# A different fixed order for the first third of a written-out instruction plan (banded attention and a gated product, one core)

## The chip, the cores and the metric

The kernel runs on one core of one Trainium2 chip. The metric is the device time of one execution in microseconds. The kernel before takes 804.42 us, the median of three runs that lie between 804.17 and 805.79 us.

## The reference

Eight batches of eight heads, head width 64. Each head has 512 local tokens and 32 global ones. A global query attends to all 544 keys of its head. A local query attends to the 32 global keys and to the local keys at most 32 positions away. The attention output, laid out as 4352 tokens of 512 features, goes through a gated product.

```python
s_g = scale * q_g @ k_all.T;      out_g = softmax(s_g) @ v_all
s_l = [scale * q_l @ k_g.T, where(|i - j| <= 32, scale * q_l @ k_l.T, -1e9)]
out_l = softmax(s_l) @ [v_g, v_l]
x = concat([out_g, out_l]) as (4352, 512)
a = x @ w1;  b = x @ w2           # 512 -> 1024
out = ((a * b) @ w3) @ w_out      # 1024 -> 1024 -> 512
```

All inputs and outputs are fp32.

## The kernel before, in words

Products that must keep fp32 precision are split: a tensor is rounded to a short "hi" part and the remainder is the "lo" part, and three matmuls (hi*hi, lo*hi, hi*lo) replace one. `hi_of` (L423) is a copy, `lo_of` (L426) a subtraction of hi from the source; nearly every hi or lo may run on more than one engine. The first batch (heads 0 to 7) uses plain fp32 matmuls instead.

The work is cut into 3878 numbered steps (`add` makes them), each a call that issues a few instructions on one engine. The ones that the prediction names:

- `sp m` on TensorE: the scores of a pair of heads (L497, 16 matmul records). `mmax n e` and `exps n e`: the masked minimum of a block of scores on VectorE (L506) and its exponential on ScalarE (L510).
- `own n`, `turn n` on VectorE: 32x32 block transposes of head n (tiles `tw`, `TT`); `eh`/`el`, `hi`/`lo`, `me`: hi and lo parts of the transposed weights (tiles `TT`, `PT`, `G`).
- `av n x` on TensorE (L637, L644): the values of head n. `cb n x`: a copy of half of its result. `sum n x` (L658): the sum of the two halves.
- `kph`/`kpl`, `vh`/`vl`: hi and lo parts of keys and values. `sg`, `cg`, `mg`: the scores of the global queries.
- `fetch`, `unit kind a e step` (L849 to L853, L423, L426): a weight block arrives packed and is unpacked in steps 0 (VectorE), 2 (ScalarE), 3 (VectorE), 4 (hi) and 5 (lo, tile `w12l`). 32 blocks of 512 KB (`raw`, three buffers) come first, then 16 of 256 KB (`w12s m e`, tile `raw_w12s`, three buffers of the ring `o`); a buffer is fetched again only after the unpacking of the block three before it has ended.
- `fold t j` (L929): the product of w3 and w_out, made on the chip. `w34h`/`w34l`: its hi and lo parts.
- `first k m s` (L795 to L797, 12 matmuls): block m of w1 (s = 0) or w2 (s = 1) for 256 tokens k; where the tokens' last pair of heads is late, nine of the 12 are a step of their own, `begin k m s`, and `first` has three. Blocks m = 4 to 7 need the four `w12s m e`. `ga`, `gb` (L805), `gh`, `gl`: the gate. `second k m` (L827 to L829): the last product. `out`, `store`: the result.

What decides the order is one string, `PLAN`: 3878 words such as `790S` or `844V`, a step's number and the engine that it runs on (P TensorE, A ScalarE, D VectorE, V GpSimd, S the DMA queue of SyncE).

```python
    for w in PLAN:
        n, e = int(w[:-1]), names[w[-1]]
        assert e in steps[n][1] and all(place[k] in seen for k in after.get(steps[n][0], ()))
```

`list_schedule` walks the string; each engine gets its steps in the order in which they stand and runs them strictly in that order. A step waits for the steps that it depends on (`after`), buffers included. The costs at the top of the file take no part once the string is written out. A few `idle_products` (L368) run on TensorE while nothing else can, at the start.

Of the kernel before, what the change touches and what calls it, by code (L numbers as in the profile page):

```python
# [30 lines left out]
def i(ap):  # L31
# [39 lines left out]
    1V 790S 386S 328S 3V 387P 791S 792P 0S 3877V 388D 390S 793D 8S 391P 5V 794A 795D 392D 797D 799D 796A 393A 12S 800A  # L71
    10A 394D 329S 13D 9D 395P 798A 396D 14A 152S 11D 397A 801P 805A 16S 808A 15D 389S 158S 803D 807V 813P 804D 806A 17D
    814D 802A 18A 809P 20S 816D 248P 818D 815A 811P 817A 19D 820D 846S 819A 258P 22A 21D 821A 810A 23D 845S 825P 827D
    24S 812A 829A 826A 828D 28S 26A 32S 249P 830D 822D 831A 25D 832A 27D 30A 399S 29D 36S 259P 847P 833P 848D 835P 31D
    850D 34A 868D 852D 834A 863A 870D 40S 854D 851A 849A 872D 250P 260P 33D 874D 853A 251P 400P 37D 855A 38A 398S 862A
    35D 875A 39D 856P 823S 859A 403S 858D 860D 261P 836D 857A 44S 330S 861A 42A 252P 864P 869A 873A 41D 48S 866P 871A
    43D 262P 46A 401D 879P 404P 52S 45D 837D 47D 49D 50A 54A 263P 159D 885A 899S 51D 883A 880A 253P 56S 405D 884D 264P
    2V 406A 900S 254P 53D 58A 55D 881A 876D 57D 331V 882A 60S 255P 265P 865D 901P 59D 886A 407D 256A 887P 257D 922D
    867A 64S 62A 266A 61D 902D 824S 877S 924D 954S 65D 888A 63D 268P 889P 269P 66A 904D 839V 154A 68S 67D 903A 408P
    270P 842V 906D 267D 923A 271P 278P 926D 72S 905A 409A 925A 916A 838V 70A 907A 69D 890A 908D 878S 272P 333V 153D 74A  # L80
    909A 928D 843A 71D 273P 402S 155D 410A 891V 76S 73D 274P 275P 844V 276D 953S 910P 913D 927A 893V 929A 80S 279P 277D
    915A 917A 894A 912A 892V 914A 280P 334V 933P 911D 918P 78A 75D 82A 77D 920P 281P 936A 332D 937A 895V 79D 840A 934D
    81D 282P 412S 896D 160A 935D 938A 288P 84S 930D 86A 164S 841D 289P 955P 413A 83D 85D 88S 87D 161D 939A 92S 919A 96S
    90A 976D 335S 283P 290P 166A 956D 958D 978D 960D 414V 957A 931S 940A 284P 94A 89D 285P 7V 959A 291P 921A 962D 91D
    98A 93D 961A 100S 941P 95D 97D 943P 942D 415P 979A 286A 336V 944A 980D 104S 416A 292P 102A 963A 165D 293P 99D 294P
# [12 lines left out]
    201D 1035A 3097A 3103P 181D 189D 1038A 1036D 1060S 422V 3104P 1064V 190A 1039D 1063A 194S 1091A 191D 1055A 450S
    3098D 1053A 1000V 1099D 1098D 442P 1056V 192A 1054V 1066S 202A 1051A 193D 195D 1052D 3105A 3099P 196A 1102A 451A
    197D 1100S 203D 3111P 1067P 434S 198A 1070P 204A 1068A 1103D 1121A 206S 199D 205D 435A 1156S 1069D 3106D 452V 207D  # L100
    1071A 1072D 208A 436V 1105A 437A 209D 443A 1122D 3100P 1096A 1073V 1094A 1104A 444D 210A 1050S 438V 211V 1132D
    3107A 3113P 1106S 218S 1131D 3112P 212S 1097V 1157P 3108D 219D 1135A 1158D 220A 1101S 3115A 1107S 1095V 214A 221D
    3109P 1188D 1133S 1136V 3110P 1160D 213D 222A 223D 1159A 224S 215D 1092A 1162D 1190D 1164D 3114P 3116D 1161A 1123S
    1093V 1078V 1163A 225D 1139S 216A 1108P 1165A 1111P 1192D 217V 1194D 226A 1109A 236S 3117A 1138A 1129A 1112A 1075V
    1134S 1110D 227D 228A 1137A 1127A 3118V 1173D 3121P 1113D 237D 1172D 230S 229V 453P 1130V 454A 455D 1128V 238A
    1140S 1125A 456A 239D 3119P 3123P 1126D 1141P 1176A 240A 457D 231D 232A 1189A 458D 242S 1144P 1177V 1142A 1174S
    1124S 1145A 244A 338S 243D 3120P 1143D 1146D 1193A 241V 466S 245D 246A 233D 247D 234A 1191A 1195A 1231P 235D 1179A
    1147V 459S 1178A 1180S 3122P 1175S 445S 1232D 3125A 1205D 339V 1206D 1234D 3124P 3135P 467V 1209A 3136P 1166A 3126D
    1074V 1148V 3127A 446A 460S 340V 1079A 1235A 1236D 1210D 1207S 3137P 341V 3139A 1238D 1167V 1262D 1076A 1264D 1181S
# [1364 lines left out]
```

## Time and profile before

| | |
|---|---|
| median of three runs | 804.42 us |
| the profiled execution | 803.93 us |
| its span | 802.2 us |
| granted TensorE clock | 1.00 throughout |
| TensorE matmuls busy | 791.2 us, 99% of the span |
| VectorE busy | 524.7 us, 65% |
| ScalarE busy | 455.2 us, 57% |
| GpSimd busy | 394.0 us, 49% |

The span runs from the first to the last instruction of the profiled execution; 1.7 us of its time lie around it. An engine's busy time leaves out waiting, issuing and branches. The shares are means over stages that differ: the first 110 us hold the folding of the weights and the first batch, up to 155 us the unpacking of the small weight blocks runs beside the first gated products, and after that the same pattern repeats.

### The profile page before, as it was taken

The page shows a single profiled execution, that of the slowest core. Times are in us where ns is not written, and L with a number is a line of the kernel's source. Part 1 is how long each engine was busy: PE and PEld are TensorE (multiplying, and loading weights), DVE is VectorE, ACT ScalarE, POOL GpSimd, SP SyncE. Part 2 cuts the span into 40 slices and gives each one's busy share as a digit, 9 for nine tenths or more (in the row PEclk, how much of TensorE's full clock was granted, in tenths as well). Part 3 has the DMA queues.
Part 4 walks back from the last instruction along what each step waited for, and adds up shares of the span by engine and source line. Part 5 has one row for each costly group of instructions (what it writes and reads, how often), then busy time and mean ns, then how long its engine had stood idle before and what let it go on. Part 6 is the DMA issues. An engine that isn't in the chain of part 4 may idle for free.

```text
span 802.2 us, 17177 instructions
## 1 busy us (share of the span) xinstructions
PE 791.2 (99%) x5608; PEld 702.8 (88%) x5608; DVE 524.7 (65%) x1498; ACT 455.2 (57%) x1300; POOL 394.0 (49%) x601
## 2 busy tenths in 40 slices
PE   9999999899999999999999999999999999999998
PEld 6656578799999999999999999999999999999997
DVE  4678889887777665677688867676576587612111
ACT  4676788766765555565656757565566554412011
POOL 2032266556656557755646656636555665412110
PEclk9999999999999999999999999999999999999999
DMA  7887688676758467565666756766664555300000
GB/s 240 283 260 239 209 245 220 177 185 160 179 152 239 122 151 188 142 187 133 161 175 171 207 153 173 182 161 173 190 164 129 156 139 154 93 27 19 10 27 26
DMA packets 195649, 128.32 MB, mean 160 GB/s; under 512 B 114472, under 2 KB 159784, under 8 KB 195560
## 3 DMA queue, kind: packets, MB, share of 16 engines
q1 hardware_dynamic: 195560, 127.23, 57.6%
q8 instruction: 44, 0.72, 0.4%
q14 instruction: 45, 0.37, 0.2%
HBM read 92.21 MB, written 34.96 MB: 159 GB/s over the span
## 4 chain that ended last, share of the span: by engine, by line
PE 89%; DVE 4%; DMA 3%; issue 2%; ACT 1%; POOL 1%; DVEq 0%; ACTq 0%; POOLq 0%
PE bp L795 8%; PE ap L795 8%; PE acc L829 7%; PE acc L828 7%; PE bp L796 7%; PE acc L827 7%; PE bp L797 7%; PE ap L797 7%; PE ap L796 7%; PE av L644 6%; PE s L497 6%; PE w L929 4%; PE av L637 2%; DMA raw_w<-in_w_t_dram 2%; PE sg L694 1%
## 5 line engine op out<-in xcount | busy, mean ns | idle before, releaser
L795 PE MATMUL bp<-x,w12h 128*128 128x256 f32 x544 | 152.7, 281 | 1.7 <-DVE g__1356 L805 0.8
L795 PE MATMUL ap<-x,w12h 128*128 128x256 f32 x544 | 153.0, 281 | 0.1
L797 PE MATMUL ap<-x,w12l 128*128 128x256 f32 x544 | 150.8, 277 | 0.4 <-DVE w12l L426 0.4
L796 PE MATMUL bp<-x,w12h 128*128 128x256 f32 x544 | 150.9, 277 | 0.0
L797 PE MATMUL bp<-x,w12l 128*128 128x256 f32 x544 | 150.9, 277 | 0.0
L796 PE MATMUL ap<-x,w12h 128*128 128x256 f32 x544 | 150.8, 277 | 0.0
L510 ACT ACTIVATE P<-P,small 128x224 f32<-128x224 f32 (+1 forms) x256 | 118.2, 463 | 24.8 <-DVE small L506 23.8
L795 PEld LDWEIGHTS bp<-x,w12h 128*128 128x128 f32 x544 | 102.2, 188 | 5.1 <-issue 1.8
L795 PEld LDWEIGHTS ap<-x,w12h 128*128 128x128 f32 x544 | 102.2, 188 | 4.9 <-issue 2.7
L796 PEld LDWEIGHTS bp<-x,w12h 128*128 128x128 f32 x544 | 102.4, 188 | 0.8
L796 PEld LDWEIGHTS ap<-x,w12h 128*128 128x128 f32 x544 | 102.3, 188 | 0.8
L797 PEld LDWEIGHTS ap<-x,w12l 128*128 128x128 f32 x544 | 102.2, 188 | 0.6 <-DVE w12l L426 0.6
L797 PEld LDWEIGHTS bp<-x,w12l 128*128 128x128 f32 x544 | 102.3, 188 | 0.0
L506 DVE CUSTOM_DVE_ANT_0 P<-s,cs 128x192 f32<-128x192 f32 (+1 forms) x256 | 82.7, 365 | 5.9 <-PE s L497 3.0
L658 DVE TENSOR_TENSOR u<-av,cb 64x352 f32<-64x352 f32 x112 | 55.8, 517 | 37.1 <-ACT cb L423 34.9
L423 ACT COPY cb<-av 64x352 f32<-64x352 f32 x73 | 31.6, 447 | 60.5 <-PE av L644 44.2
L644 PE MATMUL av<-PT,vs 128*128 128x192 f32 x448 | 61.2, 262 | 1.3 <-DVE small L724 0.7
L929 PE MATMUL w<-wo,w3f 128*128 128x512 f32 x128 | 58.4, 595 | 0.0
L644 PEld LDWEIGHTS av<-PT,vs 128*128 128x128 f32 x448 | 54.5, 163 | 3.6 <-issue 0.8
L497 PEld LDWEIGHTS s<-kq,qp 64*128 64x128 f32 x496 | 42.8, 186 | 13.7 <-issue 8.1
L426 POOL TENSOR_TENSOR TT<-TT 128x352 fp32r<-128x352 f32 x39 | 38.4, 986 | 32.2 <-ACT TT L423 14.0
L497 PE MATMUL s<-kq,qp 64*128 64x192 f32 (+1 forms) x496 | 52.5, 350 | 1.3 <-DVE u L658 0.9
(820 smaller groups left out, 1879.7 us busy)
## 6 DMA issues: line engine op xcount, KB each, us to landing
od<-tw SPq DMA_DIRECT2D x56, 256.0 KB, 3.2
own<-od SPq DMA_DIRECT2D x224, 64.0 KB, 2.3
raw_w<-in_w_t_dram SPq DMA_DIRECT2D x24, 512.0 KB, 5.1
kq<-in_kd_t_dram SPq DMA_DIRECT2D x32, 288.0 KB, 4.5
kpr<-in_kp_t_dram SPq DMA_DIRECT2D x32, 272.0 KB, 3.6
out_dram<-o_None SPq DMA_DIRECT2D x33, 256.0 KB, 2.7
qp<-in_q_t_dram SPq DMA_DIRECT2D x32, 256.0 KB, 3.8
R<-rd SPq DMA_DIRECT2D x64, 128.0 KB, 3.0
```

The lines of the kernel that those rows point to most:

```text
L497: nc.tensor.matmul(st[:, x, c : c + w], q[r, 128 * e : 128 * e + 128], k[r, o : o + w], start=(e % 2 == 0), stop=True, skip_group_check=True)
L506: nc.vector.tensor_tensor_reduce(blk(n, e), s, masks[e], -0.125, 3.0e38, ALU.add, ALU.min, T["mn", n][:, e : e + 1])
L510: nc.scalar.activation(blk(n, e), blk(n, e), AF.Exp, bias=T["mn", n][:, e : e + 1], scale=-1.0, accum_out=T["sm", n // 2][:, n % 2, e : e ...
L644: nc.tensor.matmul(av[0:r, o : o + 32 * (s1 - s0)], v[:, 0:r], PT[:, s0:s1, y, j], start=False, stop=(j % 2 == 1 and y == ys[-1]), skip_gr ...
L658: nc.vector.tensor_add(T["u", n // 2][r : r + 64, x], T.pop(("av", n, x))[r : r + 64, 0:352], T["cb", n][r : r + 64, x])
L795: nc.tensor.matmul(d, wh[:, k, c, :], x[:, 0, 0:w], start=(k == m % 2 == 0), stop=False, skip_group_check=True)
L796: nc.tensor.matmul(d, wh[:, k, c, :], x[:, 1, 0:w], start=False, stop=False, skip_group_check=True)
L797: nc.tensor.matmul(d, wl[:, k, c, :], x[:, 0, 0:w], start=False, stop=(k == 3), skip_group_check=True)
L827: nc.tensor.matmul(a, gh[:, m % 2, sl], wh[:, c], start=(m == 0), stop=False, **part)
L828: nc.tensor.matmul(a, gh[:, m % 2, sl], wl[:, c], start=False, stop=False, **part)
L829: nc.tensor.matmul(a, gl[:, m % 2, sl], wh[:, c], start=False, stop=(m in (5, 7)), **part)
L929: nc.tensor.matmul(T["w34", t], T["w3f", t, j // 4][:, j % 4], T["wo"][:, j], start=(j == 0), stop=(j == 7))
```

## The change

Only the string `PLAN` differs. The last 2499 words are the same; the first 1379 are another arrangement of the same 1379 steps. The steps after that point began at about 251 to 254 us on the five engines before.

```diff
-    1V 790S 386S 328S 3V 387P 791S 792P 0S 3877V 388D 390S 793D 8S 391P 5V 794A 795D 392D 797D 799D 796A 393A 12S 800A
-    10A 394D 329S 13D 9D 395P 798A 396D 14A 152S 11D 397A 801P 805A 16S 808A 15D 389S 158S 803D 807V 813P 804D 806A 17D
...
+    790S 1V 386S 328S 791S 3V 0S 387P 390S 792P 8S 3877V 388D 793D 795D 12S 797D 794A 796A 329S 5V 10A 391P 392D 393A
+    16S 9D 799D 800A 389S 14A 11D 394D 13D 798A 15D 20S 395P 396A 17D 18A 24S 801P 804A 397D 19D 248P 813P 806A 808A
...
```

Of the 1379 steps, 163 also change engine:

| from, to | steps | mostly |
|---|---|---|
| GpSimd to VectorE | 51 | `lo` 15, `w12` and `w12s` lo 7, `el` 6, `vl` 5, `mul` 5, `xl` 4 |
| ScalarE to VectorE | 31 | `hi` of heads 0 to 7 11, `eh` 6, `cb` 4, `sum` 3, `me` 3, `w34h` 2 |
| VectorE to GpSimd | 29 | `lo` 7, `xl` 5, `mul` 4, `gl` 4, `w12` and `w12s` lo 4 |
| ScalarE to GpSimd | 26 | `hi` 6, `me` 6, `vh` 4, `w12` and `w12s` hi 4, `kph` 3, `gh` 3 |
| GpSimd to ScalarE | 14 | `hi` 5, `me` 4 |
| VectorE to ScalarE | 12 | `hi` 5, `cb` 4 |

Steps of each engine among the 1379: TensorE 228 and 228, ScalarE 398 and 367, VectorE 405 and 446, GpSimd 147 and 137, SyncE 201 and 201.

Other moves that matter below: the fetches of `w12s 4 0` and `w12s 4 1` go from the tenth and thirteenth place of the DMA queue to behind that of `w3 6 1`. Step `sp 1`'s loads (`load q2 1`, `load k2 1`) now stand behind the fetches of `wo 2` and `wo 3` instead of ahead of them. On TensorE `begin 0 0 0` and `begin 0 0 1` go ahead of `sp 5`; the set of TensorE steps ahead of `first 0 7 0` is the same in both orders.

Between `mmax 10 0` (the first step on VectorE that reads what `sp 5` made) and the lo part of the last `w12s 7 e`, VectorE has these steps more and fewer in its queue:

```
18 more: w12s lo 4_3, 5_1, 6_1, 7_1, 7_2; lo 8_4, 8_5, 9_4, 9_5, 10_0; own 9; kpl 7; cb 10_0; el 11; eh 10; vl 4_1; me 11_0; gl 2
5 fewer: w12s lo 5_0, 5_3; lo 11_0; inv 4; gl 0
```

Ahead of `mmax 10 0` itself the VectorE queue holds 188 steps instead of 174; up to `sum 12 1`, which ended at about 168 us, it holds 310 instead of 279.

## Rows read from the trace of the kernel before

**Rows 1.** The page: the span, then busy us, share and instructions per engine.
```profile
span 802.2 us, 17177 instructions
...
PE 791.2 (99%) x5608; PEld 702.8 (88%) x5608; DVE 524.7 (65%) x1498; ACT 455.2 (57%) x1300; POOL 394.0 (49%) x601
```

**Rows 2.** Stretches: PE, PEld, DVE, ACT, POOL busy us, clock, DMA share, GB/s.
```profile
10.00:60.00 50.00, 49.18 (x214) 32.33 (x214) 36.71 (x118) 35.38 (x107) 8.11 (x16) 1.00 0.86 267
60.00:110.00 50.00, 49.62 (x196) 29.47 (x196) 41.98 (x112) 36.99 (x96) 16.18 (x20) 1.00 0.72 232
112.10:153.50 41.40, 37.38 (x276) 32.91 (x275) 36.41 (x108) 34.16 (x99) 24.70 (x37) 1.00 0.78 208
175.00:253.00 78.00, 78.00 (x594) 72.64 (x593) 60.22 (x176) 50.34 (x150) 49.08 (x69) 1.00 0.66 175
...
300.00:800.00 500.00, 498.39 (x3770) 464.07 (x3768) 298.01 (x845) 255.25 (x726) 251.21 (x387) 1.00 0.50 134
```

**Rows 3.** Waits of TensorE from 105 to 175 us: total, times, longest.
```profile
PE s L497 <- DVE u L658: 0.9, 1, 0.9
PE bp L795 <- DVE g__1356 L805: 0.8, 1, 0.8
PE bp L795 <- DVE g__1204 L805: 0.8, 1, 0.8
...
PE ap L797 <- DVE w12l L426: 0.4, 1, 0.4
```

**Rows 4.** Waits of VectorE from 112 to 153.6 us, the same columns.
```profile
DVE raw_w12s L849 <- DMA raw_w12s<-in_w_t_dram: 1.6, 2, 1.3
DVE u L658 <- ACT cb L423: 1.4, 1, 1.4
DVE g__1497 L805 <- PE bp L797: 1.1, 1, 1.1
```

**Rows 5.** Timeline of TensorE: start us, duration us, instruction, [idle before].
```profile
108.88 1.68 PE L497 MATMUL s<-kq,qp 64*128 64x192 f32 x16
110.48 0.39 PE L795 MATMUL ap<-x,w12h 128*128 128x256 f32 x1
...
154.34 0.39 PE L797 MATMUL ap<-x,w12l 128*128 128x256 f32 x1 [0.40 <-DVE w12l L426]
```

**Rows 6.** Timeline of VectorE in the same stretch.
```profile
112.07 0.36 DVE L506 CUSTOM_DVE_ANT_0 P<-s,cs 128x192 f32<-128x192 f32 x1
...
118.06 1.27 DVE L426 TENSOR_TENSOR PT<-own,PT 128x512 fp32r<-128x512 f32 x1
...
126.11 0.69 DVE L426 TENSOR_TENSOR PT<-own,PT 128x512 fp32r<-128x512 f32 x1
...
153.00 1.28 DVE L426 TENSOR_TENSOR w12l<-raw_w12s,w12h 128x256 fp32r<-128x256 f32 x2
```

**Rows 7.** VectorE groups, 112.1 to 153.5 us: count | busy us, mean ns | idle.
```profile
L426 DVE TENSOR_TENSOR w12l<-raw_w12s,w12h 128x256 fp32r<-128x256 f32 x7 | 4.3, 643 | 0.1
...
L426 DVE TENSOR_TENSOR PT<-own,PT 128x512 fp32r<-128x512 f32 x3 | 2.6, 883 | 0.0
L552 DVE STREAM_TRANSPOSE tw<-P 128x512 f32<-128x512 f32 x3 | 2.1, 696 | 0.0
...
L426 DVE TENSOR_TENSOR TT<-TT 128x352 fp32r<-128x352 f32 x2 | 1.0, 520 | 0.0
...
L426 DVE TENSOR_TENSOR gl__1439<-g__1356,gh__1393 128x512 fp32r<-128x512 f32 x1 | 0.7, 715 | 0.0
```

**Rows 8.** VectorE, then GpSimd, groups from 0 to 255 us.
```profile
L426 DVE TENSOR_TENSOR G<-TGg,G 32x32 fp32r<-32x32 f32 x6 | 2.1, 344 | 0.2
...
L426 POOL TENSOR_TENSOR PT<-own,PT 128x512 fp32r<-128x512 f32 x6 | 8.2, 1361 | 4.2 <-ACT PT L423 3.4 <-DMA raw_w12s<-in_w_t_dram 0.8
```

**Rows 9.** DMA issues: KB each, median us to landing; then SyncE's timeline.
```profile
raw_w12s<-in_w_t_dram SPq DMA_DIRECT2D x16, 256.0 KB, 5.3
...
17.53 2.35 SPq L893 DMA_DIRECT2D raw_wo<-in_wo_t_dram  x2
```

More of the change, by code (lines that the diff above doesn't have):

```diff
@@ L76 @@
[L76 to L85, printed above, removed]
@@ new lines @@
+    1030A 1022A 1057D 3093P 170S 1023D 1087A 176S 1058D 1027S 3089P 1003V 183D 171D 3092P 1005A 1033S 184A 172A 3088P
+    185D 1059S 186V 1229S 1061A 1114D 1116D 187D 173D 3090P 3094P 3095A 1115A 174A 1062D 200S 420V 1088D 1117A 177D
+    1065S 1018A 421A 1090D 1021D 178A 3101P 3102P 175D 1019D 1089A 1091A 179D 1118D 422D 1034P 1037P 3096D 180A 1120D
+    1035A 450S 188S 181V 3097V 1038A 1085A 1060S 434S 201D 1036D 1063V 1055A 1039D 1064A 202A 1098D 1000V 1099D 3098V
+    1121A 190A 3103P 1056D 442P 189D 1051A 1066S 191D 1102D 203D 194S 1100S 192V 193D 1103D 3099P 3105A 1053A 451A
@@ new lines @@
+    1076A 467A 3137P 449D 1210D 1181S 3128D 3138P 1167D 1239A 468V 342V 1235A 3140D 1170A 3129P 1247D 1197S 3130P 1168V
+    340D 1213S 1169D 1171D 1266D 1263A 1267A 1182P 1185P 3147P 1077V 1080D 1212D 3145P 3131A 1211A 3146P 1203A 1183A
+    477S 1246D 1268D 1250D 1184D 3141V 3133A 1186A 1201A 1208S 1204D 1248S 1251V 1187D 461S 1199A 3148P 1214S 1265A
+    1269A 1377S 1200D 3149A 1150A 1303S 469P 1270D 1254S 3142D 1202V 1280D 1215P 1148V 1218P 1216A 1249S 1252V 3143P
+    1219A 1217D 1281S 1244A 1253D 1153A 1220D 3144P 1151D 462A 1242V 1154V 1279D 1283D 470A 1198S 471D 1243V 1255S
@@ new lines @@
+    3174P 1400A 1401A 3195P 1402S 3189V 1428D 1367D 1390A 1365D 3196P 1368D 497A 489A 1391V 3177D 1397S 498D 1300V
+    3175A 1427D 3190D 3134S 1301A 1431A 1453P 1392A 1432D 1302D 3191P 491A 3198D 490V 1484D 1429S 1388V 1454D 1486D
+    1389D 1456D 1393V 3192P 1403S 492D 1404P 1455A 1458D 1488D 1346S 1419S 3199A 1407P 1490D 3203P 1457A 3200V 1525S
+    1369V 1374V 1460D 507P 1405D 1423V 1408A 1406D 1485A 1409D 1459A 1461A 508A 3178S 1435S 1433V 3204P 1469D 1425A
+    1371D 1489A 3201P 509D 3207A 1487A 1424D 510A 1526S 3202P 3205P 1430S 1421A 499S 1434A 1426D 1470S 3206P 1436S 511D
@@ new lines @@
+    512D 1422D 1468D 3213P 1472D 1491A 1473D 1420S 1437P 1440P 3208D 3209A 1438A 1439D 3215P 1441A 513S 1471S 1442D
+    1502D 1527P 1474V 1476S 3210V 1475D 514S 1443V 1528D 1462A 1501D 1492D 1558D 1505A 1529A 500A 1466A 1463D 1530D
+    3214P 1503S 1506V 3216P 1448D 3217A 501V 1477S 3218D 1493S 1560D 1532D 1531A 1534D 1464V 1467V 1535A 520S 1533A
+    1543D 3211P 1465V 1445V 3212P 1509S 346S 3227P 1504S 1372A 3219V 1494S 1478P 1375A 1481P 1370V 1376V 1479D 1373D
+    1510S 1508D 3220V 1480D 3228P 1499A 1482D 502A 1544S 3229P 1507A 3230P 1562D 3231A 1495A 3176S 503V 347A 1483D
@@ new lines @@
+    357A 1781A 358D 554A 356D 1666V 556A 1735D 1738D 3304P 1798D 1772S 1739V 1744V 1799S 1741D 1823P 3310D 3321P 1672V
+    568S 1771D 3323A 1797D 3311V 1801A 1854D 1856D 1824D 1826D 1828D 1773S 3322P 1758A 557V 555V 3312V 3324D 1855A
+    3329P 3313P 1829A 1802V 1825A 1759V 1762A 1805S 575A 585S 1830D 1831A 1800S 1857A 1760V 3330P 1761D 3333A 3314P
+    1827A 1788D 1763V 1858D 1740V 1839D 1789S 569S 1840S 3325V 3326D 1774P 1777P 1804A 1793A 1775D 1778A 1776D 1795A
+    3339P 3317A 1806S 576V 3340P 3331P 1803A 1790S 1859A 3315A 1779D 577P 1860D 3318S 1791V 1796D 1838D 1861A 1842A
@@ new lines @@
+    1792V 3332P 3334D 1794V 1841S 3327P 1843V 1846S 1745A 3343A 1969S 1807P 1810P 1808D 3341P 3342P 1834A 1845V 1811D
+    1742A 586V 1809D 1812D 578A 1872D 3328P 579D 1897P 587V 1873S 1813V 570A 1970S 571D 2043S 1847S 3335A 1815D 1836A
+    3336D 1832A 3316S 1844A 1837D 3349P 1833V 1874S 1898D 1900D 1899A 1871D 1875A 3350P 1835V 572A 1901A 1928D 1930D
+    573V 1929A 3337P 1932D 1902D 580S 1903A 3338P 1876V 1816A 1904D 1905A 1746D 1879S 3344D 3353A 3270S 601S 1817D
+    1848P 1851P 1862D 3351P 3352P 1933A 1818V 1934D 1863S 1913D 1743V 588P 1931A 1878V 3345A 1849D 1852A 1850D 1914S
@@ new lines @@
+    1911D 1909V 3375P 2006D 1977A 2192S 2008D 1820V 2005A 1987D 1922P 584V 3381A 1988S 1925P 1923A 3380P 1941V 1952A
+    1954S 603V 1951A 1943A 1939A 2003A 596S 3387P 3382D 3389P 612S 2007A 1938S 1942D 1926A 1944D 1986D 2009A 1924D
+    3376P 1940V 1989S 1990A 1991D 1955P 1958P 1992A 1927D 3383A 1956D 2117S 3390P 1957D 1994S 1993V 1959A 2010D 2020D
+    2021S 3384V 604P 3388P 1960D 1961D 605A 3385P 1980V 613A 606D 1984A 597A 1985D 1981D 2045P 2019D 3391A 1995S 599A
+    1982V 1983V 2022S 3397P 3398P 1966V 2076D 2046D 600V 2077A 2078D 2080D 2047A 1894V 628S 2079A 2048D 2050D 598V
@@ new lines @@
+    2098V 2038A 2120D 2122D 2121A 2036V 2124D 3423P 2126D 2125A 2150D 3362S 2054A 609D 2152D 2123A 2085S 2127A 2101S
+    366V 2055D 3424P 2056V 2096S 3425A 2057D 2058A 2153A 2135D 2059V 3406P 1968V 2154D 2136S 630V 2156D 2070P 3409A
+    2073P 2102S 2071D 3417A 3431P 2072D 639S 2100A 3418V 2089A 623S 3407D 2157A 3432P 2074D 2155A 2086S 2087A 2099V
+    2075D 2090V 2134D 364V 2088D 2137S 2138A 2091A 3426D 2151A 3419P 3420P 2092V 2158D 2168D 2139V 2103P 2106P 3427A
+    2142S 2104D 3435A 3433P 2141D 2132A 2169S 624A 3428D 2133V 2107A 2159S 2105D 626A 2039V 2265S 631P 2266S 3434P
@@ new lines @@
+    2301A 2234S 2223D 2240V 3480P 3474D 658P 2316D 2287V 2290S 2251P 667A 2285S 2254P 2189A 668D 3481P 3482P 2252A
+    2255A 2253D 2278V 2279V 3483A 2256D 2413S 2190V 2289A 659A 2257V 2291S 651A 3468P 660D 653A 652V 2288A 2280A 2306D
+    2276A 2281D 2307S 2315D 2259V 2260A 2341P 2342D 3475A 2317S 654V 3489P 3490P 3476D 2319A 2320V 2344D 2346D 661S
+    2343A 2372D 2277V 2323S 3484D 3477P 3478P 2374D 2184V 2318S 2262V 3493A 3452S 2348D 2347A 2376D 2258V 2378D 2349A
+    370S 2345A 2292P 2295P 2293D 3485A 3491P 2294D 2324S 2321D 2322A 2356D 2313A 3486V 2487S 2296A 669P 2297D 3492P
@@ new lines @@
+    2598D 2513S 2566D 2499D 2599A 3553P 3554P 2568D 720S 2567A 2597A 2540S 2570D 690V 2569A 2528D 3556D 2500V 2501D
+    3561P 3562P 2502A 2571A 2503V 691V 2565A 2579D 3542P 3565A 692V 2580S 710A 3502S 2514P 3545D 3557V 2517P 2600D
+    2543V 2546S 2535A 2536V 3558V 2544A 2578D 378S 3563P 3564P 3543D 2601A 2531A 2710S 2515A 2529S 2412V 3559P 2582A
+    3560P 2532D 704S 2518A 2533A 2534V 2547P 2516D 2581S 2519D 711V 3566D 2583V 3567A 2550P 2548A 2586S 3568V 3571P
+    2595A 3544S 2530S 2574A 2549D 2584A 712P 2551D 2552D 3572P 2553D 713A 2572A 705V 707V 3569P 721A 706V 2587S 714D
@@ new lines @@
+    2637P 2573D 2784S 3573P 3574P 2602D 2612D 2585V 722V 2611D 2613S 2603S 2668D 3570P 2615A 2638D 2575V 2576A 383S
+    2640D 2669A 2485A 3575A 2480V 2709S 2642D 2670D 2577V 2588P 2591P 2643A 2672D 2674D 2671A 708D 2641A 2616D 2486V
+    3576D 2619S 2589A 3581P 2614S 2644D 723P 2639A 3546S 2607V 2590D 2618A 3577V 2592A 2593D 724A 3578V 3582P 3583P
+    715S 2555V 2609A 725D 2645A 2620S 2608V 379A 2653D 2654S 3585A 3584P 726A 2617D 2652D 2558D 736S 727D 3595P 2604S
+    2556A 2673A 728D 729S 2605V 3579P 2656D 2606D 2783S 3586D 2675A 2655S 3580P 3587A 2686D 2610V 2621P 2624P 2657V
@@ new lines @@
+    3698P 2928V 2984S 2925V 3038D 2946A 3040D 3694V 3013A 3014D 3015A 3041A 2947D 3699P 3700P 2944V 3011A 771D 2855A
+    3023D 2945V 3695P 785S 3701A 2924V 3024S 3702D 2850V 2958P 2961P 2959A 3707P 2987D 2990S 2988D 2977V 2978V 2975A
+    3022D 3039A 2974S 3708P 2929A 2976D 2979A 3026A 3042D 3044D 3709P 3043A 3045A 3696P 3027V 3030S 3046D 2980D 3025S
+    3056D 2991P 2994P 2856V 2960D 3703A 3704D 3710P 786V 3057S 2926A 2962A 2963D 3047S 3711A 3029D 3018A 3028A 3031S
+    3705P 788V 3712D 2992A 3684S 789V 2995A 3055D 3019V 3079A 787D 3059A 3016A 3060D 3717P 3718P 3020A 3017D 3063S
@@ L267 @@
+    3850P 3852D 3861A 3846P 3853A 3859P 3854V 3860P 3862D 3863A 3855P 3856P 3864D 3865P 3866P 3871A 3867P 3868P 3869P
+    3870P 3873D 3875A 3872S 3874S 3876S
 """.split()
```

316 lines of the change are left out of this document (132 added, 184 removed).

## The prediction

> **What bounds the kernel now.** The page's first part comes first: TensorE is busy for 791.2 us of a span of 802.2, VectorE for 524.7 [rows 1]. A reordering takes nothing from those 791.2 us; it can only move the other 11. So the second view is the busy time by stretch, which says where they lie [rows 2]. From 175 to 253 us TensorE is busy for 78.00 of 78.00, and from 300 to 800 for 498.39 of 500, at a clock of 1.00: nothing is to be won there, and a delay that reaches 175 us is not made up afterwards. The stretch from 112.1 to 153.5 us is the weak one: TensorE is busy for 37.38 of 41.40 us, so about 4 us are lost. In the same stretch VectorE is busy for 36.41 us and ScalarE for 34.16. The third view is the waits of TensorE: its longest ones from 105 to 175 us were ended by VectorE (`sum`, `gb` twice, a `w12l`: 0.9, 0.8, 0.8, 0.4) [rows 3]. The fourth is VectorE's own waits there: 1.6 us for weight blocks, 1.4 for ScalarE, 1.1 for TensorE, together 4.1 of the 5.0 us in which it isn't busy [rows 4, 2]. The reader is to see two engines that nearly take turns: TensorE waits for VectorE, and VectorE has about 4 us of waits of its own left to fill. That stretch decides this change.
>
> **The change, part by part.** No work is added. 163 steps change engine, and VectorE gets 41 steps more. TensorE's order changes too, but the set of steps ahead of `first 0 7 0` is the same, so the time at which that step can start measures the stretch.
>
> *VectorE between `mmax 10 0` and the last `w12s 7` lo.* It gets 18 steps and loses 5. By the durations of the same tiles on VectorE: five `w12l` at 0.643 make 3.2 us; `lo 10 0` 0.88; `gl 2` and `kpl 7` at 0.715 make 1.4; `own 9` 0.70; `el`, `eh`, `cb` and `vl` at 0.520 (the tile `TT`; no row for the other three, and near it) make 2.1; five small ones at 0.344 make 1.7 [rows 7, 8]. Sum 10.0. The five that go: `gl 0` 0.72, `lo 11 0` 0.88, two `w12l` 1.29, `inv` about 0.4 (an estimate, near the small row): 3.3. Net 6.7 us. These means hold prolonged ones: three `PT` subtractions took 0.883 on average [rows 7], an undisturbed one 0.69 [rows 6], a factor of 0.78. With it on everything the net would be 5.2. I take 5.5 of 5.2 to 6.7, nearer the undisturbed durations.
>
> *When that work can begin and when it must end.* `mmax 10 0` needs `sp 5`, which ended at 110.48, where the first gated product starts [rows 5]. In the new order two `begin` steps stand ahead of `sp 5`: 18 matmuls, at 37.38 / 276 = 0.135 us each in this stretch [rows 2], so 2.4 us. `sp 5` then ends at 112.9, and with a handoff of 0.1 (the one at 154.28 to 154.34, below, took 0.06) VectorE starts `mmax 10 0` at 113.0 at the earliest, 0.9 later than the 112.07 of before [rows 6]. Before, the work ended at 153.00 + 1.28 = 154.28, and TensorE's `w12l` wait at 154.34 [rows 5, 6]. New: 113.0 + 36.4 (busy before) + 5.5 = 154.9, plus whatever VectorE waits or is slowed, w. Against 154.3 that is 0.6 + w later. Before, w was 5.0 (41.40 - 36.41). If all of it were filled by the added work the change would cost 0.6 us here; if none, 5.6.
>
> *What w will be.* The wait for weight blocks (1.6) sits in a loop that the order doesn't shorten: three buffers, 5.3 us to a landing [rows 9], and a block is fetched only after the lo part of the one three before, which a later VectorE ends later. The wait for `cb` (1.4) is ScalarE's, which loses work, and the wait for TensorE (1.1) should shrink, for TensorE is then the later partner. The 0.9 us of slots between instructions stay. I take w = 3.2, so 3.8 us at this point.
>
> *Ahead of the stretch.* `mmax 10 0` has 188 VectorE steps ahead of it instead of 174. VectorE was busy for 36.71 of 50 and 41.98 of 50 us there [rows 2], so most of the extra 14 steps (5.9 us at 0.42 each, from the net above) fall into idle time: 21 us are free, 8 of them in the later half. TensorE is not waiting there (49.62 of 50), so the cost is below what is left uncovered: between 0 and 2 us, and I take 0.8 because the free time lies mostly in the early half. The moved fetches of the two first small blocks lie under TensorE's folding, and the first gated product that reads them stands behind 110 us: cost 0, and up to 1.9 if the 0.5 MB, at 267 KB per us [rows 2], puts off a `raw` block by its whole time.
>
> *Behind it.* Up to `sum 12 1` VectorE has 310 steps instead of 279; 31 at 5.5 / 13 = 0.42 are 13 us more. Counted whole, with the idle time of before unfilled, that would be 13 us late, which is the upper end of what the queue can cost; it is not what I expect, because idle time gives way first. From 175 us VectorE is busy for 60.22 of 78, so it falls no further behind. One wait of 0.4 us near 171 may go.
>
> *Steps that leave ScalarE and GpSimd.* They shorten queues that don't end TensorE's long waits: at nothing. A lo part takes 0.88 instead of 1.36 us [rows 7, 8], which helps a chain by 0.5 us each where GpSimd was last; that is counted under the rival below.
>
> Sum: 3.8 + 0.8 = 4.6 us. The profiled execution took 803.93, so 808.5; the median of the three runs is 0.5 above the profiled one, so 809.0.
>
> **A rule against a row.** The two `lo` subtractions of one shape took 1.27 and 0.69 us [rows 6]. The Trainium skill, SBUF — State Buffer, "Who interferes with whom", says why that can be: a VectorE instruction with two SBUF inputs and a GpSimd instruction that reads SBUF use one shared interface, and the later one is blocked. By that rule fewer GpSimd steps mean fewer long subtractions on VectorE, and more subtractions on VectorE mean more that can be hit. The row fits it but doesn't show the other engine's part. If every prolongation went, the three `PT` subtractions would give back about 0.6 us, and the sum would be 808.4 instead of 809.0.
>
> **The rivals.**
> - *No change.* The added work fills the idle time of VectorE exactly: w near 0, nothing lost ahead. For it: 5.0 us are idle, 5.5 are added. Against it: the idle time is made by partners that stay. Then 0.6 here and 0 to 1 ahead: 805.0 to 806.0, so 805.5.
> - *Faster.* The waits that VectorE ends were latency, not load: lo parts on the faster engine, and TensorE has other steps in between. All of rows 3 is 2.9 us, and the stretch loses 4.0 [rows 2]; if half of the 4.0 and the 0.4 near 171 go, 804.4 - 2.4 = 802.0. Against it: 5.5 us more work on the engine that ends the waits.
> - *Much slower.* The loop of three buffers follows VectorE: each late lo part puts off a fetch that takes 5.3 us [rows 9], three rounds lie in the stretch, and the queue's whole surplus shows. It decides when VectorE falls behind by more than a fetch has in hand. 13 us: 817.4.
> - *The start decides.* `load k2 1` now waits behind two fetches that issued over 17.53 to 19.88 [rows 9], and `sp 1` waits for it: 2.35 us later. If TensorE pays it whole, with VectorE's waits filled: 804.4 + 0.6 + 2.35 = 807.4, slower too, with another place. Against it: other steps and the idle products stand there.
>
> **How the numbers follow.** What a measurement can tell here is about 0.2%, 1.6 us. Forecast: 0.54. No change: 0.18. Faster: 0.17. Much slower: 0.06. The start: 0.05. Faster by over 0.2%: 0.17; within: 0.18; slower: 0.54 + 0.06 + 0.05 = 0.65. The forecast's own range is 806 to 814 (w from 1 to 5, 0 to 2 ahead, and some of the queue's surplus). The range of 802.5 to 814 takes in "no change" and the start, and leaves out most of "faster" and "much slower".
>
> **What would show it.** In the new profile: VectorE busy for 41 us or more between `sp 5` and `first 0 7 0`, with idle time of 3 to 4 us; the waits of TensorE from 105 to 175 us ended by VectorE and 4 us longer in total; GpSimd and ScalarE less busy by 300 us; a dense TensorE behind 180 us. The prediction is wrong if TensorE's idle time before 175 us hasn't grown: then the added steps replaced waits, and w was the step that failed; or if the growth lies ahead of 110 us or on a DMA.

## The result, and the profile after

The changed kernel takes 814.58 us (median of four runs, 813.58 to 815.52) against 804.39: a ratio of 1.0123, 95% interval 1.0105 to 1.0140. The sign was as forecast, the size was not: 10.2 us instead of 4.6, just above the range's upper end of 814. And little of it lies where the prediction put it.

The page of the changed kernel: the span, then busy us, share and instructions of each engine.

```profile
span 812.9 us, 17180 instructions
...
PE 800.0 (98%) x5608; PEld 709.4 (87%) x5608; DVE 541.3 (67%) x1540; ACT 444.2 (55%) x1269; POOL 382.4 (47%) x590
```

The reader is to see that the same 5608 matmuls are busy for 8.8 us longer than in [rows 1], while what the span holds beside them grew by 1.9 only (12.9 against 11.0). That points to slower matmuls more than to waits, though short waits can hide in it: a matmul's record is 0.28 us long where the next one begins after 0.113. The stretches of [rows 2] in the changed kernel:

```profile
10.00:60.00 50.00, 48.65 (x208) 31.49 (x207) 40.13 (x124) 32.38 (x95) 4.95 (x10) 1.00 0.87 268
60.00:110.00 50.00, 50.00 (x200) 30.27 (x198) 44.93 (x119) 36.17 (x97) 14.91 (x18) 1.00 0.74 233
112.10:153.50 41.40, 37.87 (x280) 32.94 (x277) 39.14 (x119) 32.89 (x97) 19.61 (x34) 1.00 0.77 204
175.00:253.00 78.00, 76.49 (x571) 70.50 (x571) 62.30 (x181) 45.78 (x135) 44.52 (x67) 1.00 0.67 168
...
300.00:800.00 500.00, 500.00 (x3752) 465.87 (x3751) 300.45 (x850) 255.36 (x729) 251.77 (x388) 1.00 0.50 134
```

Two lines are out of the expected. From 300 to 800 us, where both kernels run the same instructions in the same order, TensorE is busy throughout at a clock of 1.00 and gets through 3752 matmuls instead of 3770. And from 175 to 253, where it was dense before, it now misses 1.5 us. The stretch from 112 to 153, the prediction's weak one, is no worse (37.87 busy, was 37.38).

Two points in the timeline of TensorE cut the difference into three pieces: the start of `first 0 7 0`, which needs the last of the small weight blocks, and that of `first 3 2 0`, among the last of the changed words. First before, then after:

```profile
153.09 0.39 PE L795 MATMUL ap<-x,w12h 128*128 128x256 f32 x1
...
251.77 0.30 PE L795 MATMUL ap<-x,w12h 128*128 128x256 f32 x1
```

```profile
153.63 0.39 PE L795 MATMUL ap<-x,w12h 128*128 128x256 f32 x1
...
256.40 0.30 PE L795 MATMUL ap<-x,w12h 128*128 128x256 f32 x1
```

Up to the first point 0.5 us are lost, between the two 4.1 (102.8 instead of 98.7), and behind the second 6.1 (812.9 - 256.4 = 556.5 against 802.2 - 251.8 = 550.4), with the same order and an empty list of TensorE's waits. From the second point to the end (stretch, TensorE's busy time, matmuls, clock, DMA), before and after:

```profile
251.80:802.20 550.40, 546.59 (x4140) 1.00 0.51 136
```

```profile
256.40:812.90 556.50, 552.70 (x4140) 1.00 0.50 134
```

The same 4140 matmuls are busy for 6.1 us longer, and 3.8 us lie beside them in both. The waits of TensorE in the second piece (154 to 256 us: total, times, longest) are mainly at `av` steps; the one by `issue`, time in which the engine waited for nothing that the profile shows, is at `av 14`:

```profile
PE av L637 <- DVE G L426: 1.7, 2, 1.0
PE av L637 <- issue: 0.7, 1, 0.7
PE ap L797 <- DVE w12l L426: 0.3, 1, 0.3
```

The largest piece, the third, is a lower speed of the matmuls themselves. The step `first 4 7 0` shows it, an even chunk of tokens, 12 matmuls; the first and the last, before and after:

```profile
314.81 0.28 PE L795 MATMUL ap<-x,w12h 128*128 128x256 f32 x1
...
316.05 0.28 PE L797 MATMUL ap<-x,w12l 128*128 128x256 f32 x1
```

```profile
320.19 0.28 PE L795 MATMUL ap<-x,w12h 128*128 128x256 f32 x1
...
321.48 0.28 PE L797 MATMUL ap<-x,w12l 128*128 128x256 f32 x1
```

Eleven distances take 1.24 and 1.29 us: 113 ns a matmul before, 117 to 118 after. In the odd chunk behind it (`first 5 1 0`) the changed kernel is as quick as the one before:

```profile
328.78 0.28 PE L795 MATMUL ap<-x,w12h 128*128 128x256 f32 x1
...
330.02 0.28 PE L797 MATMUL ap<-x,w12l 128*128 128x256 f32 x1
```

Call a distance of 117 ns or more slow and one of 114 or less quick. From the third chunk on, the even ones are slow in 98% of their distances or more, and the odd ones quick in 58 to 85% (before, from the fourth chunk on: quick in 78 to 89%, even and odd). Even and odd chunks keep their tokens in two rings of tiles, tags `x0` and `x1` (L777). A pool places a tag where its first tile is asked for, so the order of the steps decides the layout. Before, the keys' tag `kph` (2176 bytes, which is 2048 and 128) came behind both rings; in the changed order it comes between them. So all 11 x tiles began 1344 bytes behind a multiple of 2048, and now the five of `x0` begin at 1472. (For the last chunk that ring also lends two tiles to the gate, which 18 of the 822 matmuls of `second` read.)

### The profile page after: what moved, and what is told of

Its sections match the earlier page's. It is cut to its first block, busy times and chain, and to the rows that moved or that the text cites. A ratio compares the mean times of both kernels' runs of the same rounds, so it can differ in the third digit from the quotient of the medians.

```text
span 812.9 us, 17180 instructions
## 1 busy us (share of the span) xinstructions
PE 800.0 (98%) x5608; PEld 709.4 (87%) x5608; DVE 541.3 (67%) x1540; ACT 444.2 (55%) x1269; POOL 382.4 (47%) x590
## 4 chain that ended last, share of the span: by engine, by line
PE 87%; DVE 4%; DMA 3%; ACT 2%; issue 1%; POOL 1%; SPq 1%; POOLq 0%; DVEq 0%; ACTq 0%
PE bp L795 7%; PE ap L795 7%; PE acc L827 7%; PE acc L829 7%; PE acc L828 7%; PE bp L797 7%; PE bp L796 7%; PE ap L797 7%; PE ap L796 7%; PE av L644 6%; PE s L497 5%; PE w L929 5%; PE av L637 2%; PE sg L694 2%; DMA raw_wo<-in_wo_t_dram 1%; DMA own<-od 1%
## 5 line engine op out<-in xcount | busy, mean ns | idle before, releaser
L795 PE MATMUL bp<-x,w12h 128*128 128x256 f32 x544 | 153.5, 282 | 0.7 <-DVE g__1214 L805 0.4
L510 ACT ACTIVATE P<-P,small 128x192 f32<-128x192 f32 (+1 forms) x256 | 118.3, 463 | 37.9 <-DVE small L506 37.0
L644 PE MATMUL av<-PT,vs 128*128 128x192 f32 x448 | 60.6, 262 | 0.0
L644 PEld LDWEIGHTS av<-PT,vs 128*128 128x128 f32 x448 | 54.5, 162 | 1.7
L426 POOL TENSOR_TENSOR TT<-TT 128x352 fp32r<-128x352 f32 x33 | 32.9, 996 | 33.4 <-ACT TT L423 16.1
```

What stands on the lines that cost most here:

```text
L510: nc.scalar.activation(blk(n, e), blk(n, e), AF.Exp, bias=T["mn", n][:, e : e + 1], scale=-1.0, accum_out=T["sm", n // 2][:, n % 2, e : e ...
L644: nc.tensor.matmul(av[0:r, o : o + 32 * (s1 - s0)], v[:, 0:r], PT[:, s0:s1, y, j], start=False, stop=(j % 2 == 1 and y == ys[-1]), skip_gr ...
L795: nc.tensor.matmul(d, wh[:, k, c, :], x[:, 0, 0:w], start=(k == m % 2 == 0), stop=False, skip_group_check=True)
```

## The experiments

**Is it the place of the tiles?** First the changed kernel again, unaltered.

> The changed kernel once more, unaltered, as the yardstick of the next two runs. In its first trace 6.1 of the 10.7 us that the span grew lie behind 256 us, where the order of both kernels is the same: the matmuls of the gated product come 117.7 ns apart in the even chunks of tokens and 113.3 ns apart in the odd ones. If that belongs to the program (its addresses in SBUF), this run shows the same split by chunk, even chunks from the third on slow nearly throughout, and about 814.5 us. If it is chance of an execution, the slow chunks are others and the time moves by some us.

814.26 us, ratio 1.0124 (1.0109 to 1.0140), with the same chunks slow. It belongs to the program.

Then the changed kernel with the ring put back, and the kernel before with the ring moved:

```diff
         if part == 0:
+            if not X:
+                p1.tile([128, 2, 256], F32R, tag="x0", name="x0_first", bufs=NX[0])
             X[key] = p1.tile([128, 2, 256], F32R, tag=f"x{e}",
```

> The changed order with one unused tile more: it makes the ring of x tiles of the even chunks (tag x0) be placed right behind that of the odd ones, so that all 11 begin 1344 bytes behind a multiple of 2048, as in the kernel before; in the changed kernel those five begin at 1472. Theory (address): the even chunks run at 113.3 ns a matmul too, and the time falls by 6 to 7 us, to about 808; what stays, 3 to 4 us over the kernel before, is the waits ahead of 256 us. Rival (the phase in which TensorE's stream enters, or the load of the other engines): no change, 814.5.

```diff
             X[key] = p1.tile([128, 2, 256], F32R, tag=f"x{e}",
...
+            if len(X) == 1:
+                p1.tile([128, S], F32R, tag="kph", name="kph_first")
```

> The kernel before, its order untouched, with one unused tile of the keys' ring (kph, 2176 bytes) that pushes the x0 ring to 1472 behind a multiple of 2048, as in the changed kernel. Theory (address): slower by 6 to 8 us, 811 to 812, with the even chunks at 117.7 ns. Rival (phase or load): 804.4 as before.

807.93 us (1.0051, 1.0038 to 1.0063) and 811.09 us (1.0088, 1.0075 to 1.0101), as the theory of the address said. The pages, of the changed order with all tiles at 1344, then of the old order with `x0` at 1472:

```profile
span 805.8 us, 17180 instructions
...
PE 791.5 (98%) x5608; PEld 702.2 (87%) x5608; DVE 541.7 (67%) x1540; ACT 444.7 (55%) x1269; POOL 381.9 (47%) x590
```

```profile
span 808.9 us, 17177 instructions
...
PE 796.8 (99%) x5608; PEld 708.1 (88%) x5608; DVE 525.1 (65%) x1498; ACT 455.2 (56%) x1300; POOL 393.7 (49%) x601
```

TensorE's busy time goes with the place of the tiles (791 and 797 to 800), whichever order runs. What the order itself costs is the other 3.6 us (807.9 - 804.3): in its span of 805.8, 14.3 us lie beside the matmuls instead of 11.0.

**The operand's place by itself.** The core of the loop, shortened; from group to group only the places vary:

```python
GROUPS = [(0, x) for x in range(0, 512, 8)]     # place of weights, of the moving operand, in units of 4 bytes
...
for k in range(4):
    matmul(d, wh[k], hi[k]); matmul(d, wh[k], lo[k]); matmul(d, wl[k], hi[k])
```

> Leaves out the whole computation but 6624 matmuls of the gated product's shape (128x128 weights, 256 columns, fp32r), in its pattern of hi and lo, on copies of one input. Groups of 36 matmuls differ in the place of the moving operand within 2048 bytes (steps of 32 bytes, in two orders) and of the weights within 512. Theory (address): the distance of two matmuls depends on the place of the moving operand, with 113 ns at 1344 and 118 at 1472, the same in both orders. Rival (phase): the distance doesn't follow the place, or it follows the group before. If it follows the difference of the two operands' places, the third set of groups shows that.

Two groups of this run, the moving operand at 1344 and then at 1472, weights where `w12h` has them (128 behind a multiple of 512):

```profile
171.91 0.28 PE L36 MATMUL acc<-x,w 128*128 128x256 f32 x1
...
172.47 0.28 PE L38 MATMUL acc<-x,w 128*128 128x256 f32 x1
```

```profile
188.81 0.28 PE L38 MATMUL acc<-x,w 128*128 128x256 f32 x1
...
189.52 0.28 PE L38 MATMUL acc<-x,w 128*128 128x256 f32 x1
```

Five distances in 0.56 us (0.112) and six in 0.71 (0.118). No other engine works there, so none can be the reason. Over all places of the moving operand, with the weights fixed, mean ns from one matmul to the next by the distance of the two operands (moving minus weights, modulo 256 bytes). Left out are the run's first group, when the engine had just begun, and the first six distances of every group, in which the pace still changes over (119, 120, 119, 123, 118, 114 ns in one that then ran at 113); the two orders of the groups agree within 1.1 ns for every place:

```
distance    0      32     64     96    128    160    192    224
ns      119.9   117.2  117.8  120.0  118.7  117.3  113.3  118.4
```

It repeats every 256 bytes. When the weights move too, the quick place moves with them, so it is the distance that counts: 192 is quick. 1344 less 128 is 192 (modulo 256), 1472 less 128 is 64. In the third set, though, four of the 14 groups at a distance of 192 stayed at 117.8: the distance allows the quick pace and doesn't ensure it.

**Where the order's 3.6 us lie.** The two orders hold the same steps ahead of 154 us, but for five, so they can be cut there and crossed:

```diff
 PLAN: ... 1231P 459S 235D 247D
-      1232D 1147V 446A 1196D ...   # changed order goes on
+      466S 1147V 1178A 3122P ...   # order and engines of before
```

> The changed kernel with all x tiles at 1344 (a_x_even, 807.9 us), up to the last lo part of w12s 7 in the changed order (827 steps, about 154 us), all behind it in the order of the kernel before, on its engines. The two orders have the same steps ahead of that point but for five. Theory (rear): a_x_even reached first 0 7 0 at 153.0 us, as the kernel before did (153.1), and lost its 3.6 us behind, at av 12, av 14 and av 16, which waited for VectorE; so this gives 804.3, give or take 0.8. Rival (front, the prediction's own step): VectorE's surplus of steps ahead of 154 us is what shows behind it, and 807 to 808 stays.

> The other half of that pair: the kernel before up to the last lo part of w12s 7 (824 steps), the rest in the changed order on its engines, all x tiles at 1344. Theory (rear): 807.5 to 808.5, as a_x_even. Rival (front): 804.4, as the kernel before.

803.81 us (0.9996, 0.9986 to 1.0005) and 809.20 us (1.0057, 1.0042 to 1.0071; 0.7 us above the range expected). The loss is behind 154 us, wholly; the front, where the prediction put it, costs nothing. In the changed order with the tiles put back, this is the largest of the waits behind that point, on TensorE, then on VectorE:

```profile
164.52 0.40 PE L831 MATMUL acc<-w34h,gl__1807 128*128 128x512 f32 x1
166.10 0.40 PE L637 MATMUL av<-G,vgs 128*128 128x288 f32 x1 [1.19 <-DVE G L426]
```

```profile
163.78 0.24 DVE L426 TENSOR_TENSOR QG<-qgr,QG 64x128 fp32r<-64x128 f32 x1
164.74 0.80 DVE L426 TENSOR_TENSOR PT<-TGr,PT 128x128 fp32r<-128x128 f32 x1 [0.72 <-POOL PT L423]
165.57 0.48 DVE L426 TENSOR_TENSOR G<-TGg,G 32x32 fp32r<-32x32 f32 x1
```

`av 12` waits 1.19 us for a lo part on VectorE, which itself waited 0.72 for a hi part that had gone from ScalarE to GpSimd. Two more waits follow, 0.75 us by `issue` at `av 14` (184 us) and 0.95 for another lo part on VectorE at `av 16` (206 us). Is it the engines or the order?

```diff
-... 1209D ... 1167D ... 1169D ... 1358D     # eh 13, lo 12 0, lo 12 4, el 17
+... 1209A ... 1167V ... 1169V ... 1358V     # 39 words in all
```

> a_x_even with its order as it is, but the 39 steps behind 154 us that had gone to VectorE back on the engine of before (28 to GpSimd, 11 to ScalarE). Theory (rear, by VectorE's load): TensorE's waits for VectorE at av 12, av 14 and av 16 go, and 804.5 to 806 is left. Rival (rear, by the order of the steps): the waits stay or move to GpSimd, 807 to 809.

808.36 us (1.0050, 1.0037 to 1.0062): my theory of VectorE's load fails. The waits move to GpSimd (total, times, longest; L635 and L642 are L637 and L644 of before):

```profile
PE av L635 <- POOL G L424: 2.8, 2, 1.4
PE av L642 <- DVE PT L424: 0.4, 1, 0.4
```

So order and engines were taken apart fully, all 86 words behind 154 us in each:

> a_x_even with its order as it is, but all 86 steps behind 154 us that had changed engine back on the engine of before. With the next run it makes a pair: order and engines of the rear apart. Theory (order): the changed order has fewer matmuls on TensorE between sp 9 and av 18 (172 instead of 190, 2 us less) and between sp 10 and av 20 (184, 196), so the waits stay there whichever engine does the parts: 806.5 to 808.5. Rival (engines): 803.8 to 805, as with the rear of before.

> a_then_b (803.8 us: changed order up to 154 us, the order of before behind it) with the engines of the changed kernel behind 154 us, in the order of before. Theory (order): 804 to 805. Rival (engines): 806.5 to 808, with waits of TensorE at av 12, av 14 and av 16.

809.89 us (1.0069, 1.0055 to 1.0084; 1.4 us above the range expected) with the changed order on the old engines, and 804.36 us (1.0003, 0.9992 to 1.0013) with the old order on the new engines. The order decides, and the moves between engines behind 154 us cost nothing in the right order. Is it TensorE's own order (as I had expected from the matmuls between scores and values)?

> a_x_even (807.9 us) with one queue changed: behind 154 us TensorE has its steps in the order of the kernel before, while VectorE, ScalarE, GpSimd and SyncE keep the changed order and engines. Theory (TensorE's own order: too few matmuls between a pair's scores and its values): 803.8 to 805.5, the waits at av 12, av 14 and av 16 gone. Rival (the order in which VectorE, ScalarE and GpSimd make the parts): 807 to 809 or more, the waits stay.

823.64 us (1.0238, 1.0215 to 1.0261), with waits of up to 3.3 us:

```profile
PE ap L795 <- ACT as__2778 L801: 3.3, 1, 3.3
PE av L635 <- DVE G L424: 2.3, 2, 2.1
PE s L495 <- DVE u L656: 1.8, 1, 1.8
```

That theory fails too. TensorE in the old order waits for ScalarE, VectorE and GpSimd, whose queues still have the changed one; its order alone isn't the cause. That the queues have to fit one another as a set is my reading. The opposite, one queue of another engine in the old order, was not run, so which of them starts the delay stays open.

**Did VectorE's added work ahead of 154 us cost anything?** The 16 steps back on their old engines, in the order of `a_then_b`:

```diff
-... 452D ... 1093D ... 3118D     # kpl 7, lo 10 0, gl 2
+... 452V ... 1093V ... 3118V     # 16 words in all
```

> a_then_b (803.8 us) with the 16 steps between mmax 10 0 and the last lo part of w12s 7 that VectorE had taken over (13 of GpSimd, 3 of ScalarE) back on their engines of before; the order stays the changed one. The prediction's step (VectorE's added work costs 3.8 us in this stretch) expects 800 to 801. Theory (the work filled VectorE's idle time, and its other steps got shorter): no gain, 803.5 to 805, or a loss where GpSimd now ends a wait.

803.63 us (0.9986, 0.9975 to 0.9997), beside 0.9996 (0.9986 to 1.0005) with them on VectorE. The intervals overlap; a gain of 3 us is excluded. (This interval lies just below 1, by 0.14% in the middle.)

All of these in one table: us from the start to `first 0 7 0`, from there to `first 3 2 0`, and the rest, each from the one profiled execution.

```
kernel             x0 at   order ahead / behind 154   front   rear    rest
before             1344    before / before            153.1    98.7   550.4
changed            1472    changed / changed          153.6   102.8   556.5
after_again        1472    changed / changed          153.6   102.3   556.4
a_x_even           1344    changed / changed          153.0   102.3   550.5
b_x_odd            1472    before / before            153.8    98.7   556.4
a_then_b           1344    changed / before           153.5    97.9   550.7
b_then_a           1344    before / changed           154.9   101.2   550.5
a_even_back        1344    changed / changed          152.5   102.6   550.5
a_even_allback     1344    changed / changed          154.1   103.6   550.8
b_rear_a_engines   1344    changed / before           155.4    98.7   550.4
ab_front_back      1344    changed / before           155.2    97.7   550.4
a_rear_b_tensor    1344    changed / TensorE before   153.1   117.8   550.8
```

The last column has two levels, 550.4 to 550.8 and 556.4 to 556.5, and follows the place of `x0` alone. The rear, but for `a_rear_b_tensor`, has two levels, 97.7 to 98.7 and 101.2 to 103.6, and follows the order behind 154 us. The front spreads over 3 us whatever stands in it (153.0 and 155.4 for one and the same front), so it says nothing finer: the profiled execution of `b_rear_a_engines` is the longest of its twelve (806.47, median 804.36).

**Can more be had from the places?** The other shapes first:

> Leaves out the whole computation but 2304 matmuls on copies of one input, in groups of 36 that differ in the columns of the moving operand (512 as in second, 192 and 224 as in av, 256 as in first), and in the places of both operands within 256 bytes. Theory (address): what counts is the distance of the two places; 512 columns come 226.7 ns apart at a distance of 192 and up to 233 elsewhere (second in the kernel before, at a distance of 64: 228.5). Rival: only matmuls of 256 columns depend on it. The last set repeats the fast distance behind groups of every other distance, to see whether a slow group is carried on.

It has 96 groups, 3456 matmuls. 512 columns, left out what was left out above: 226.7 ns at a distance of 0, 228.8 to 229.0 at 64, 232.7 to 234.4 elsewhere. So these depend on the places too, but I had expected the quick one at 192, where they take 233.3 or 233.4. 192 and 224 columns: 111.5 to 111.9 wherever they lie. At 256 columns the distance of 192 gave 113.3 or 113.4 in all 20 groups here, behind a slow group too. The kernel before has its 512-column weights `gh` and `gl` at a distance of 64, so a gap was put ahead of them, and one to bring x back to its own:

```diff
+            if not X:
+                p1.tile([128, 48], F32, tag="gap1", name="gap1")
             X[key] = p1.tile([128, 2, 256], F32R, tag=f"x{e}",
...
+                    if tag == "gh":
+                        p1.tile([128, 16], F32, tag="gap0", name="gap0")
                     T["w3f", a, h] = pool.tile(
```

> The kernel before with 64 unused bytes ahead of the tiles gh and gl and 192 ahead of the x tiles: x stays at the distance of 192 from its weights, and gh and gl (weights of second) come to a distance of 0 from w34 (its moving operand) instead of 64. By the map of shapes its 512-column matmuls take 226.7 ns instead of 228.8; 136 steps of second have 12 of them or, with those that lie alone left out, some 800 to 1600 in all: 1.5 to 3 us, so 801.5 to 803. Rival (the map doesn't carry over to a kernel with stalls and other steps between): 804.3.

> The same two gaps in a_then_b, which tied with the kernel before (803.8 us). If the gain of the gaps is that of the map, 801 to 802.5: faster than both kernels. Rival: 803.8.

A miss, and the wrong way: 807.20 us (1.0033, 1.0022 to 1.0043) and 806.38 us (1.0024, 1.0014 to 1.0034). `first 14 3 0` before, then with the gaps (lines lie two further on in that kernel):

```profile
706.43 0.28 PE L795 MATMUL ap<-x,w12h 128*128 128x256 f32 x1
...
707.67 0.28 PE L797 MATMUL ap<-x,w12l 128*128 128x256 f32 x1
```

```profile
706.45 0.28 PE L797 MATMUL ap<-x,w12h 128*128 128x256 f32 x1
...
707.75 0.28 PE L799 MATMUL ap<-x,w12l 128*128 128x256 f32 x1
```

Eleven distances take 1.24 us and 1.30: with x at its good distance the stream is slow again in this chunk (6% quick distances, 88% before) and in the last two (none), and in the even chunks from the fifth on it is quick in 54 to 66% instead of 81 to 88%. Within `second` the most common distance fell from 229 to 227 ns, as the map has it, but the mean only from 227.6 to 227.2. So the distance alone doesn't say which pace a stream has. What else decides, no run here shows: the gaps changed the matmuls of `second`, which the stream follows, but they also moved x and its weights by 256 bytes together. No version beats the kernel before clearly; `a_then_b` ties with it.

## Why the prediction was wrong

- **"A reordering takes nothing from those 791.2 us."** This is the step that failed, and it lost 6 to 7 us: by the crossed pair 814.3 - 807.9 = 6.3 and 811.1 - 804.3 = 6.8. The words of the plan decide not only when a step runs but where the pools put its tiles, and TensorE's pace hangs on that. Neither the forecast nor a rival had it. The Trainium skill, SBUF — State Buffer, "Who interferes with whom", gives TensorE two read ports, one for the moving operand and one for the weights, independent of each other, and says that it never waits for anyone. Taken as a promise of one pace it would have said the same as I did; the map differs (113.3 ns against 117.2 to 120.0 with no other engine at work), and the measurement decides.
- **The main term, 3.8 us up to `first 0 7 0`.** Measured: 0.5 in the changed kernel, nothing with the tiles put back (153.0 against 153.1), each in one execution. The medians say it better: `a_then_b`, with the whole changed front, ties with the kernel before, and `ab_front_back` shows that the 16 steps cost nothing. VectorE from the start of `mmax 10 0` to the end of the last `w12s 7` lo part (stretch, busy time, instructions, clock, DMA), before and after:

```profile
112.07:154.29 42.22, 37.22 (x108) 1.00 0.77 207
```

```profile
113.17:155.19 42.02, 39.83 (x119) 1.00 0.78 205
```

  The start was forecast well (113.2 against 113.0). The sum after it left out 0.8 us, for its 36.4 are the busy time up to 153.5 and the work that it counts ended at 154.28. Two of its parts were too large: busy time grew by 2.6 us, not by 5.5, and the idle time w fell from 5.0 to 2.2, where it was set at 3.2. In part the work grew by less because the steps that stayed got shorter: those that both stretches hold took 38.6 us in sum instead of 40.2. The `w12l` and `PT` subtractions of [rows 7] after:

```profile
L426 DVE TENSOR_TENSOR w12l<-raw_w12s,w12h 128x256 fp32r<-128x256 f32 x6 | 3.0, 501 | 0.3 <-ACT w12h L423 0.3
...
L426 DVE TENSOR_TENSOR PT<-own,PT 128x512 fp32r<-128x512 f32 x3 | 2.0, 677 | 0.0
```

  501 instead of 643 ns and 677 instead of 883, with GpSimd busy for 19.61 us there instead of 24.70. The subtraction `lo 8 0` took 1.27 us before [rows 6], with these two of GpSimd beside it, and 0.68 after, with GpSimd idle:

```profile
118.05 0.74 POOL L426 TENSOR_TENSOR vs<-vr,vs 128x256 fp32r<-128x256 f32 x1
118.75 1.18 POOL L426 TENSOR_TENSOR x<-u,x 128x256 fp32r<-128x256 f32 x1
```

```profile
119.54 0.68 DVE L426 TENSOR_TENSOR PT<-own,PT 128x512 fp32r<-128x512 f32 x1
```

  In both traces up to 255 us, the eleven subtractions of this shape on VectorE during which GpSimd stood still took 0.64 to 0.69 us; the four that took over 1.2 all had GpSimd instructions beside them (of four others with some, three were not longer). The rule of the Trainium skill that the prediction weighed (SBUF — State Buffer, "Who interferes with whom": VectorE with two SBUF inputs against GpSimd's reads) would have it so, and this trace agrees, though no run here isolates it. The prediction priced it at 0.6 us. And of the waits of VectorE [rows 4], 4.1 us in three, this is what is left:

```profile
DVE cb L423 <- PE av L644: 0.5, 1, 0.5
DVE u L658 <- ACT cb L423: 0.4, 1, 0.4
DVE w12l L426 <- ACT w12h L423: 0.3, 1, 0.3
```

  The 1.6 us for weight blocks, which I took for a loop that the order doesn't shorten, are gone. TensorE's idle time from 112.1 to 153.5 us did not grow (3.5 us, was 4.0), the sign that had been named for a w that fails.
- **Ahead of the stretch, 0.8 us.** Not seen: `mmax 10 0` began 0.2 us behind the time that the sum has without this term, and `first 0 7 0` at the same time with the tiles put back.
- **Behind the stretch, nothing ("it falls no further behind").** Wrong: about 3.6 us are lost between 154 and 256 us, at waits for `av 12`, `av 14` and `av 16` (at 166, 184 and 206 us). A mean busy share (60.22 of 78) says nothing of whether the one part that is wanted next is late. But the rival "much slower" isn't borne out either: it was the loop of three buffers, and with the changed order throughout, the waits of TensorE behind 156 us are listed for parts of the heads on VectorE or, moved there, on GpSimd, or by `issue`, and none for a weight block. The price came from the order of the queues, not from VectorE's surplus: the new engines in the old order run at 804.4. Which queue begins the delay is open.
- **What the sign rested on.** Slower was right by luck: 3.6 us came from another place and reason than the forecast's, and 6 to 7 from one that was not thought of.

## What to carry to other kernels

When a program's order changes, compare the addresses of its hot tiles as well as its timeline: here a tag's first use moved by a few steps and shifted a ring by 128 bytes, and the matmuls that read it ran 4% slower (117.8 ns instead of 113.3) for the rest of the program. The page gives the hint: the same number of matmuls with more busy time at the same clock. And judge a changed order by cutting and crossing it with the old one where both hold the same steps; here three stretches came apart cleanly that way, and one queue of the one order did not fit the four of the other.

## What the runs showed of the hardware that was not expected

- The time from one 128x256 fp32r matmul to the next depends on the distance of its two operands in SBUF modulo 256 bytes: 113.3 ns at 192, 117.2 to 120.0 elsewhere (`map_moving`). For 512 columns it is 226.7 at 0, 228.8 at 64, and about 233 elsewhere; for 192 and 224 columns there is no dependence (111.5 to 111.9; `map_shapes`).
- The quick distance is needed but not enough: a stream can run for a whole chunk at about 117.8 ns at the right distance (`b_gh64`, and four of 14 groups of `map_moving`, while all 20 of `map_shapes` were quick). What decides it stays open.
